# Attention, soft mixture of experts and a feed-forward block on one core: q and k loaded eight tokens to a partition, one head on each half of the partitions

## The chip, the core and the metric

The kernel runs on one core of a Trainium2 chip. A time is the device time of one execution, in microseconds (us), and the figure of a kernel is the median of its runs. Profiles are of one execution each. TensorE is PE below (PEld its weight loads), VectorE DVE, ScalarE ACT, GpSimd POOL, and SP is the queue that issues every DMA of this kernel.

## What is computed

Three blocks follow one another, all in float32: attention inside chunks of 64 tokens (8 batches, 8 heads, 576 tokens, head size 64), a soft mixture of 8 experts with 4 slots each, and a feed-forward block whose activation is the softplus.

```python
scores = scale * np.matmul(q_c, k_c.transpose(0, 1, 2, 4, 3))   # per chunk of 64
scores = scores - np.max(scores, axis=-1, keepdims=True)
attn = np.exp(scores)
attn = attn / (np.sum(attn, axis=-1, keepdims=True) + 1e-09)
out = np.matmul(attn, v_c)
...
logits = x @ phi                       # x: 4608 x 512
d = np.exp(logits - logits.max(0, keepdims=True))   # over the tokens
d /= d.sum(0, keepdims=True) + 1e-09
slot_input = d.T @ x                   # 8 experts x 4 slots x 512
slot_out[e] = np.maximum(slot_input[e] @ w1[e], 0.0) @ w2[e]
c = np.exp(logits - logits.max(1, keepdims=True))   # over the slots
c /= c.sum(1, keepdims=True) + 1e-09
x = c @ slot_out
...
h = x @ w_in
g = np.maximum(h, 0.0) + np.log1p(np.exp(-np.abs(h)))
out = g @ w_out
```

## The kernel before

**Units and loads.** The 4608 tokens are nine groups of 512, and a group has four units, each of two heads. A pair of units (`pr`, 18 of them) shares one load of q and one of k: 512 tokens of four heads, 1 MB for both. A batch has 576 tokens, so a group may lie across a batch boundary. `runs` (line 286) then cuts it in two pieces, whose first token in the group is a multiple of 64. Groups 0 and 8 are not cut, group 4 is cut into 256 and 256 tokens, the other six unevenly (64+448, 128+384, 192+320 and the reverse). `load_q` (line 295) issues one DMA for each piece of q and of k. In its tile `[128, 4, 4, D]` a partition holds four tokens of each of the four heads, so one packet is 4 x 64 floats, 1 KB, and 512 tokens fill all 128 partitions; a piece of 64 tokens fills 16 of them. There are two buffers each for q and k, and three for v, whose load (`load_v`, line 303) goes in packets of 256 bytes.

**A unit's steps.** `st_A` (line 424) turns one head's q and k: two transposes of 128x128 for each, every one over two tokens of each partition, into one bank of PSUM. `st_B` copies that bank on ACT into the tile `T` (line 442), in which the head has its 64 rows and the tokens stand in order. `st_S` (line 455) takes the scores of a chunk from `T`; softmax, the product with v, its transposes and the logits against `phi` follow. While this runs, the feed-forward weights `w_in` are loaded and rounded on DVE and POOL, and some expert weights are loaded ahead.

**What sets the order.** Every step of attention is given to `issue` (line 131), a small planner: it has a table of costs by engine (`COST`, line 106) and of buffers (`BUF`), and writes the steps out in the order in which its own clock would start them. That order is then fixed on every engine, SP's queue among them. `COST` has 3.4 for a load of q and k and 0.55 for a step `st_A`. A DMA on the queue waits until the buffer is free (the last transposes of the load two before), and until the DMA eight places ahead of it has landed, since eight semaphores go round. After attention the expert weights stream through the same queue (`hps` and `sops` are the two products), and the feed-forward block runs from a table of steps written out by hand (`MID`).

```python
# line 428 to 433, one head's transposes
for rr in range(2):
    nc.tensor.transpose(
        o[:, rr, :], t[:, 2 * (u % 2) + h, 2 * rr:2 * rr + 2, :].rearrange(
            "p r d -> p (r d)"), ident)
```

Of the kernel before, what the change touches and what calls it, by code (L numbers as in the profile page):

```python
# [8 lines left out]
F32 = mybir.dt.float32  # L9
# [174 lines left out]
def kernel(  # L184
# [12 lines left out]
    nc = tc.nc  # L197
    B, H, S, D = q.shape
# [21 lines left out]
    ident = const.tile([128, 128], F32, name="ident")  # L220
# [54 lines left out]
    rp_ = raw_ctx.enter_context(tc.tile_pool(name="raws", bufs=1, reuse_waits="tile"))  # L275
# [10 lines left out]
    def runs(t0, n):  # L286
        done = 0
        while done < n:
            b, s = divmod(t0 + done, S)
            step = min(n - done, S - s)  # L290
            yield done, step, b, s
            done += step


    def load_q(src, t, pr, hs=range(4)):
        G, h0 = pr // 2, 4 * (pr % 2)
        for off, n, b, s in runs(G * GT, GT):
            nc.sync.dma_start(
                out=t[off // 4:(off + n) // 4, hs[0]:hs[-1] + 1],
                in_=src[b, h0 + hs[0]:h0 + hs[-1] + 1, s:s + n, :].rearrange(  # L300
                    "h (p r) d -> p h r d", r=4))

    def load_v(t, pr):
        G, h0 = pr // 2, 4 * (pr % 2)
# [95 lines left out]
    def tr_tile(i):  # L400
        return psa.tile([128, 512], F32, tag=f"tr{i}", name=f"tr{i}")
# [3 lines left out]

    def st_l(pr):
        def f(e, held):
            ts = [rp_.tile([128, 4, 4, D], F32, tag=f"{nm}{held[nm, pr]}", name=nm)
                  for nm in "qk"]
            V["qk", pr] = ts  # L410
            for hs in (range(4),) if pr else (range(2), range(2, 4)):
                for src, t in zip((q, k), ts):
                    load_q(src, t, pr, hs)
        return f
# [9 lines left out]
    def st_A(u, h):  # L424
        def f(e, held):
            p = V["A", u, h] = tr_tile(held["tr", ("A", u, h)]).rearrange("x (i t) -> x i t", i=2)
            for i, t in enumerate(V["qk", u // 2]):
                o = p[:, i].rearrange("x (p rr) -> x rr p", rr=2)
                for rr in range(2):
                    nc.tensor.transpose(  # L430
                        o[:, rr, :], t[:, 2 * (u % 2) + h, 2 * rr:2 * rr + 2, :].rearrange(
                            "p r d -> p (r d)"), ident)
        return f

    def st_B(u, h):
# [228 lines left out]
    for u in range(NU):  # L664
        G, hp = divmod(u, HP)
        pr = u // 2
# [38 lines left out]
    for i in range(16):  # L705
        r = 2.0 * i + 3
# [21 lines left out]
    for i, (c, nms_, sls) in enumerate(ends):  # L728
# [4 lines left out]
        for sl in sls:  # L733
            n = next(n for n in home_of if home_of[n] == sl)
# [18 lines left out]
    for a in range(4):  # L753
# [5 lines left out]
        out=phi, in_=moe_phi.rearrange("(k p) s -> p k s", p=128)), rank=2.5)  # L759
# [9 lines left out]
        out=nM[:, 0], in_=nmr.rearrange("p g s -> p s g"), axis=AX.X, op=ALU.min)  # L769
# [10 lines left out]
        out=rep4w, in0=rep4[:, 0, :], scalar1=wc, scalar2=None, op0=ALU.mult)  # L780
# [22 lines left out]
    for kt in range(KD):  # L803
        nc.tensor.matmul(
            out=sp[:, kt, :], lhsT=acc[:, kt * 128:(kt + 1) * 128], rhs=rep4w,
# [119 lines left out]
    hps = psh.tile([128, 2, 512], F32, name="hps")  # L925
# [293 lines left out]
```

## Time and profile before

| what | value |
|---|---|
| median of 3 runs | 726.34 us (725.5 to 728.25) |
| the profiled execution | 725.14 us, its span 723.4 us |
| mean granted clock of TensorE | 0.969 |
| PE busy | 653.4 us (90%) |
| PE weight loads | 514.9 us (71%) |
| DVE busy | 414.4 us (57%) |
| ACT busy | 345.6 us (48%) |
| POOL busy | 336.7 us (47%) |
| DMA | 89.06 MB in 85440 packets |

A share of busy time is a mean over the whole span, in which the blocks follow each other with different loads on the engines; so the page's 40 slices (18 us each) come first, then the same table for chosen stretches. A matmul's busy time includes its way through the array, so a row of matmuls is read by the times at which they start. "DMA share" is the mean busy share of the 16 DMA engines; it goes over 1 because packets overlap. 1 GB/s is 1 KB per us.

### The profile page before, as it was taken

Reading aid. Unit: us, or ns where it says so; the run is one execution under the profiler, and the core shown is the slowest. Engines: PE = TensorE matmul, PEld = TensorE weight load, DVE = VectorE, ACT = ScalarE, POOL = GpSimd, SP = SyncE. Lnnn points to the kernel's source line nnn. Section 1 sums busy time; section 2 is a strip of 40 time slices with the busy share of each in tenths; the row PEclk is TensorE's granted clock in tenths of the full one; section 3 lists DMA queues with packets and bytes.
Section 4 is the critical chain, followed back from the end, with each engine's and each line's share of the span. In section 5 each row is a group of like instructions: output and inputs, shape, how many; then the busy total and the mean of one; then the engine's idle time right before and its main releaser. Section 6 shows DMA issues by size and latency. Waiting matters only on the chain.

```text
span 723.4 us, 14073 instructions
## 1 busy us (share of the span) xinstructions
PE 653.4 (90%) x5811; PEld 514.9 (71%) x5811; DVE 414.4 (57%) x598; ACT 345.6 (48%) x526; POOL 336.7 (47%) x222
## 2 busy tenths in 40 slices
PE   7779768878689687999999999999999999999997
PEld 6666556766444354877778888888888888888886
DVE  2768668778748558798785544444444444444430
ACT  5879667778522334465445333333333333333340
POOL 3647556556222423868755444434443433333340
PEclk9999999999979999999999999999999999999999
DMA  9999999999989993000002111000010010100101
GB/s 238 231 225 259 212 217 241 257 234 289 381 317 376 390 396 122 1 1 0 1 0 59 43 46 30 30 13 17 30 30 29 1 30 29 30 1 29 30 30 29
DMA packets 85440, 89.06 MB, mean 123 GB/s; under 512 B 41856, under 2 KB 60288, under 8 KB 85376
## 3 DMA queue, kind: packets, MB, share of 16 engines
q1 hardware_dynamic: 85376, 88.16, 43.8%
q8 instruction: 46, 0.75, 0.5%
q14 instruction: 18, 0.15, 0.1%
HBM read 78.71 MB, written 9.44 MB: 122 GB/s over the span
## 4 chain that ended last, share of the span: by engine, by line
PE 62%; DMA 15%; DVE 8%; issue 5%; ACT 4%; POOL 4%; SPq 1%; POOLq 0%; ACTq 0%; DVEq 0%
PE trm L1143 15%; PE trm L1141 15%; PE trm L1145 15%; DMA k<-in_k_dram 9%; PE ph L1090 4%; DMA w6b<-in_moe_w_dram 3%; PE tr L430 3%; ACT T L442 2%; PE hps L938 2%; DMA w3b<-in_moe_w_dram 1%; PE X L507 1%; PE S L455 1%; DMA vb<-in_v_dram 1%; POOL cvl L380 1%; PE tr L542 1%
## 5 line engine op out<-in xcount | busy, mean ns | idle before, releaser
L1124 POOL TENSOR_TENSOR g<-hTm,g 128x1024 fp32r<-128x1024 f32 (+1 forms) x48 | 112.7, 2348 | 143.7 <-ACT g L1120 143.7
L1109 ACT ACTIVATE hTm<-hTm 128x1024 f32<-128x1024 f32 (+2 forms) x51 | 51.5, 1010 | 160.3 <-DVE hTm L1103 160.3
L1103 DVE TENSOR_SCALAR hTm<-ph 128x1024 uint32<-128x1024 uint32 (+2 forms) x51 | 59.0, 1159 | 84.7 <-PE ph L1090 84.7
L442 ACT COPY T<-tr 64x512 f32<-64x512 f32 x144 | 90.2, 626 | 28.6 <-PE tr L430 26.7
L1124 POOL TENSOR_TENSOR g<-siT,g 128x1024 fp32r<-128x1024 f32 x24 | 58.1, 2422 | 62.3 <-ACT g L1120 62.3
L380 POOL TENSOR_TENSOR cvl<-cvl,cve 128x512 f32<-128x512 f32 x30 | 40.6, 1355 | 94.9 <-DVE cve L364 70.6
L1113 DVE SCALAR_TENSOR_TENSOR hTm<-ph,hTm 128x1024 f32<-128x1024 f32 (+2 forms) x51 | 59.1, 1159 | 39.6 <-ACT hTm L1109 39.6
L1109 ACT ACTIVATE siT<-siT 128x1024 f32<-128x1024 f32 x24 | 25.5, 1061 | 85.1 <-DVE siT L1103 85.1
L1090 PEld LDWEIGHTS ph<-cT,Tc 128*128 128x128 f32 x288 | 44.1, 191 | 17.0 <-issue 3.8
L1103 DVE TENSOR_SCALAR siT<-ph 128x1024 uint32<-128x1024 uint32 x24 | 29.3, 1222 | 42.9 <-PE ph L1090 42.9
L1090 PE MATMUL ph<-cT,Tc 128*128 128x256 f32 x288 | 47.8, 287 | 6.3 <-DVE hTm L1113 2.5
L1120 ACT CAST g<-hTm 128x1024 fp32r<-128x1024 f32 (+2 forms) x51 | 50.3, 988 | 2.2 <-DVE hTm L1113 2.2
L430 PE MATMUL tr<-ident,k 128*128 128x128 f32 x144 | 31.0, 300 | 14.3 <-DMA k<-in_k_dram 13.0
L1113 DVE SCALAR_TENSOR_TENSOR siT<-ph,siT 128x1024 f32<-128x1024 f32 x24 | 29.3, 1222 | 20.3 <-ACT siT L1109 20.3
L382 POOL TENSOR_TENSOR cvl<-cvl,cva 128x512 f32<-128x512 f32 x28 | 36.7, 1313 | 8.4 <-DVE cvl L380 6.5
L430 PE MATMUL tr<-ident,q 128*128 128x128 f32 x144 | 32.0, 307 | 8.5 <-DMA q<-in_q_dram 6.4
L549 DVE COPY xT<-tr 128x512 f32<-128x512 f32 x36 | 24.7, 686 | 20.8 <-PE tr L542 20.5
L467 DVE TENSOR_REDUCE nm<-S 128x8 f32<-128x512 f32 x36 | 24.8, 688 | 17.5 <-PE S L455 16.9
L455 PE MATMUL S<-T 64*64 64x64 f32 x1152 | 27.6, 234 | 6.6 <-DVE P L473 3.7
L430 PEld LDWEIGHTS tr<-ident,k 128*128 128x128 f32 x144 | 19.5, 155 | 17.4 <-DMA k<-in_k_dram 8.8
L542 PE MATMUL tr<-ident,x 128*128 128x128 f32 x144 | 24.1, 293 | 7.3 <-ACT T L442 3.8
L455 PEld LDWEIGHTS S<-T 64*64 64x64 f32 x1152 | 23.2, 146 | 9.8 <-issue 5.3
(364 smaller groups left out, 1730.3 us busy)
## 6 DMA issues: line engine op xcount, KB each, us to landing
g<-in_moe_w_dram SPq DMA_DIRECT2D x12, 1024.0 KB, 10.8
vb<-in_v_dram SPq DMA_DIRECT2D x64, 128.0 KB, 7.2
d<-in_moe_w_dram SPq DMA_DIRECT2D x5, 1024.0 KB, 13.7
out_dram<-ts SPq DMA_DIRECT2D x18, 256.0 KB, 2.1
out_dram<-ts SPq DMA_DIRECT2D x36, 128.0 KB, 2.3
w0a<-in_moe_w_in_dram SPq DMA_DIRECT2D x8, 512.0 KB, 5.9
w0b<-in_moe_w_in_dram SPq DMA_DIRECT2D x8, 512.0 KB, 7.1
q<-in_q_dram SPq DMA_DIRECT2D x4, 448.0 KB, 6.6
```

What stands on the lines that cost most here:

```text
L430: nc.tensor.transpose(o[:, rr, :], t[:, 2 * (u % 2) + h, 2 * rr:2 * rr + 2, :].rearrange("p r d -> p (r d)"), ident)
L442: on(e)(out=t[64 * h:64 * h + 64, :, r2, :], in_=p[64 * r2:64 * r2 + 64])
L455: nc.tensor.matmul(out=sp[64 * o:64 * o + 64, b, 64 * i:64 * i + 64], lhsT=qT[64 * h:64 * h + 64, cs], rhs=kT[64 * h:64 * h + 64, cs], sta ...
L1090: nc.tensor.matmul(out=ph(n, a, b)[:, j - a, :], lhsT=K["Tc"][:, f * 128:(f + 1) * 128], rhs=K["cT"][:, t * TT:(t + 1) * TT], start=True, ...
L1103: nc.vector.tensor_scalar(out=scratch(n, a, b).bitcast(U32), in0=ph(n, a, b).bitcast(U32), scalar1=0x80000000, scalar2=None, op0=ALU.bitwi ...
L1109: nc.scalar.activation(out=y, in_=y, func=AF.Softplus)
L1113: nc.vector.scalar_tensor_tensor(out=y, in0=ph(n, a, b), scalar=0.0, in1=y, op0=ALU.max, op1=ALU.add)
L1120: nc.scalar.copy(out=V["gs", n][:, 0, a:b], in_=scratch(n, a, b))
L1124: tt(eng)(out=s[:, 1, a:b], in0=scratch(n, a, b), in1=s[:, 0, a:b].bitcast(F32), op=ALU.subtract)
L1141: nc.tensor.matmul(out=po, lhsT=s[:, 0, j, ts_], rhs=wr[:, hs], start=(n in begin and j == 0), stop=False)
L1143: nc.tensor.matmul(out=po, lhsT=s[:, 0, j, ts_], rhs=wr[:, ls], start=False, stop=False)
L1145: nc.tensor.matmul(out=po, lhsT=s[:, 1, j, ts_], rhs=wr[:, hs], start=False, stop=(j == 3 and (n in part_end or n in sum_end)))
```

## The change

q and k stand in the tile `[128, 2, 8 * D]`. A partition holds eight tokens of two heads, one of each of the load's two units; the first head of each unit (`h = 0`) is on partitions 0 to 63, the second on 64 to 127. A packet is 8 x 64 floats, 2 KB. `load_q` issues two DMAs for each piece, one for each half. `st_A` turns one head with four transposes for q and four for k, each of 64 partitions and 128 columns against a 64x64 identity. The columns of the PSUM bank mean the same tokens as before, so all later steps are as they were. The planner's costs are as before, and so is the order in which it writes the steps.

```diff
-    def load_q(src, t, pr, hs=range(4)):
+    def load_q(src, t, pr, hps=range(2)):
         G, h0 = pr // 2, 4 * (pr % 2)
+        hs = slice(hps[0], hps[-1] + 1)
         for off, n, b, s in runs(G * GT, GT):
-            nc.sync.dma_start(
-                out=t[off // 4:(off + n) // 4, hs[0]:hs[-1] + 1],
-                in_=src[b, h0 + hs[0]:h0 + hs[-1] + 1, s:s + n, :].rearrange(
-                    "h (p r) d -> p h r d", r=4))
+            for h in range(2):
+                p0 = 64 * h + off // 8
+                nc.sync.dma_start(
+                    out=t[p0:p0 + n // 8, hs],
+                    in_=src[b, h0:h0 + 4, s:s + n, :].rearrange(
+                        "(hp h) (p r) d -> h p hp (r d)", h=2, r=8)[h, :, hs])
...
     def st_l(pr):
         def f(e, held):
-            ts = [rp_.tile([128, 4, 4, D], F32, tag=f"{nm}{held[nm, pr]}", name=nm)
+            ts = [rp_.tile([128, 2, 8 * D], F32, tag=f"{nm}{held[nm, pr]}", name=nm)
                   for nm in "qk"]
             V["qk", pr] = ts
-            for hs in (range(4),) if pr else (range(2), range(2, 4)):
+            for hs in (range(2),) if pr else (range(1), range(1, 2)):
...
             for i, t in enumerate(V["qk", u // 2]):
-                o = p[:, i].rearrange("x (p rr) -> x rr p", rr=2)
-                for rr in range(2):
+                o = p[:, i].rearrange("x (p rr) -> x rr p", rr=4)
+                hs = slice(64 * h, 64 * h + 64)
+                for rr in range(4):
                     nc.tensor.transpose(
-                        o[:, rr, :], t[:, 2 * (u % 2) + h, 2 * rr:2 * rr + 2, :].rearrange(
-                            "p r d -> p (r d)"), ident)
+                        o[:, rr, :], t[hs, u % 2, 128 * rr:128 * rr + 128], ident[hs, hs])
```

SP's queue before, at the load of the fourth pair (group 1, cut 64+448) with the `w_in` load behind it; a size is partitions x heads x floats, and `DMAHW0` to `DMAHW7` are the eight DMA semaphores:

```order
L298 DMA q<-in_q_dram 16x4x256 [waits DMAHW2_49,PE_49]
L298 DMA q<-in_q_dram 112x4x256 [waits DMAHW3_49]
L298 DMA k<-in_k_dram 16x4x256 [waits DMAHW4_49,PE_49]
L298 DMA k<-in_k_dram 112x4x256 [waits DMAHW5_49]
L341 DMA w0a<-in_moe_w_in_dram 128x1024 [waits DVE_49,DMAHW6_49,Activation_49,Pool_49]
```

The same place of the queue now:

```order
L302 DMA q<-in_q_dram 8x2x512 [waits DMAHW4_49,PE_49]
L302 DMA q<-in_q_dram 8x2x512 [waits DMAHW5_49]
L302 DMA q<-in_q_dram 56x2x512 [waits DMAHW6_49]
L302 DMA q<-in_q_dram 56x2x512 [waits DMAHW7_49]
L302 DMA k<-in_k_dram 8x2x512 [waits DMAHW0_49,PE_49]
L302 DMA k<-in_k_dram 8x2x512 [waits DMAHW1_49]
L302 DMA k<-in_k_dram 56x2x512 [waits DMAHW2_49]
L302 DMA k<-in_k_dram 56x2x512 [waits DMAHW3_49]
L345 DMA w0a<-in_moe_w_in_dram 128x1024 [waits DVE_49,DMAHW4_49,Activation_49,Pool_49]
```

Each transfer has become two, of half the partitions that it had, and the load goes once round the eight semaphores. In all, 66 transfers of q and k become 132.

Before, the same queue at group 4, whose loads were cut in the middle, each piece on one half of the partitions:

```order
L298 DMA q<-in_q_dram 64x4x256 x2
L298 DMA k<-in_k_dram 64x4x256 x2
L307 DMA vb_111<-in_v_dram 128x4x64 x4
L341 DMA w0b<-in_moe_w_in_dram 128x1024
```

PE before, at the first scores (S) and the transposes of the next unit (`tr` is the PSUM bank; a size is that of the output):

```order
L455 MATMUL S<-T 64x64 x32
L430 MATMUL tr_234<-ident,q 128x128 x2
L430 MATMUL tr_234<-ident,k 128x128 x2
L488 MATMUL tr_241<-ident,P 128x128 x4
L430 MATMUL tr_251<-ident,q 128x128 x2
L430 MATMUL tr_251<-ident,k 128x128 x2
```

The same place now:

```order
L459 MATMUL S<-T 64x64 x32
L435 MATMUL tr_256<-ident,q 128x64 x4
L435 MATMUL tr_256<-ident,k 128x64 x4
L492 MATMUL tr_267<-ident,P 128x128 x4
L435 MATMUL tr_277<-ident,q 128x64 x4
L435 MATMUL tr_277<-ident,k 128x64 x4
```

Nothing has changed its place; each head has eight transposes of half the width instead of four, 576 in all instead of 288.

## Rows read from the trace of the kernel before

**Rows 1.** The page's 40 slices of the span, in tenths; GB/s moved.
```profile
PE   7779768878689687999999999999999999999997
...
PEclk9999999999979999999999999999999999999999
DMA  9999999999989993000002111000010010100101
GB/s 238 231 225 259 212 217 241 257 234 289 381 317 376 390 396 122 1 1 0 1 0 59 43 46 30 30 13 17 30 30 29 1 30 29 30 1 29 30 30 29
```

**Rows 2.** Three stages: stretch, length, busy us (instructions) by engine, PEclk, DMA share, GB/s.
```profile
0.00:180.00 180.00, 142.11 (x2912) 112.64 (x2913) 125.57 (x273) 135.94 (x249) 100.85 (x102) 0.93 1.05 240
180.00:277.00 97.00, 75.85 (x870) 42.85 (x872) 62.75 (x125) 33.59 (x68) 31.55 (x25) 0.90 1.00 372
277.00:723.40 446.40, 435.47 (x2035) 359.39 (x2027) 226.05 (x202) 176.02 (x211) 204.29 (x96) 1.00 0.08 22
```

**Rows 3.** Line 430, the transposes of q and k: PE idle before it, until what.
```profile
its engine sat idle before it (us, times) until:
  DMA k<-in_k_dram: 21.8, 18
...
  DMA q<-in_q_dram: 10.0, 10
```

**Rows 4.** The same columns as rows 2, the 160 us inside attention.
```profile
20.00:180.00 160.00, 127.21 (x2706) 99.90 (x2699) 118.77 (x262) 123.80 (x230) 94.75 (x74) 0.94 1.06 240
```

**Rows 5.** Stretches with the packets of an uncut load (groups 0 and 8).
```profile
1.80:7.10 5.30, 4.00 (x19) 3.24 (x17) 0.00 (x0) 1.42 (x3) 2.31 (x15) 1.00 0.98 252
8.80:11.90 3.10, 1.07 (x34) 0.74 (x32) 1.32 (x2) 3.02 (x6) 0.00 (x0) 1.00 1.08 372
163.60:168.20 4.60, 3.81 (x106) 2.88 (x106) 4.36 (x10) 4.28 (x9) 4.35 (x4) 1.00 1.15 335
171.30:176.30 5.00, 3.84 (x33) 2.34 (x33) 4.78 (x10) 4.88 (x9) 1.14 (x1) 1.00 0.99 279
```

**Rows 6.** The two loads of group 4, each piece on one half of the partitions.
```profile
73.60:80.30 6.70, 4.02 (x106) 2.87 (x106) 4.25 (x11) 4.27 (x7) 6.14 (x5) 1.00 1.16 204
83.30:90.50 7.20, 6.10 (x145) 4.28 (x141) 5.30 (x13) 5.67 (x14) 3.12 (x3) 0.92 1.14 217
```

**Rows 7.** First and last of the twelve unevenly cut loads, and their sum.
```profile
15.30:22.10 6.80, 5.28 (x133) 4.35 (x135) 5.22 (x12) 6.38 (x12) 1.36 (x1) 0.94 1.06 252
...
151.10:157.40 6.30, 5.95 (x143) 4.51 (x138) 5.50 (x15) 4.87 (x12) 2.98 (x3) 0.87 1.10 236
sum 79.00, PE 64.89 PEld 50.52 DVE 63.20 ACT 63.84 POOL 46.21; mean PE 5.41 PEld 4.21 DVE 5.27 ACT 5.32 POOL 3.85
```

**Rows 8.** Line 298, the issues of q and k: ns min/median/max, and time to landing.
```profile
L298 SPq DMA_DIRECT2D k<-in_k_dram x33: 314/459/1618, 1.2 to 169.7; - x33
...
DMA to landing us min/median/max: 2.9/6.9/11.0
```

**Rows 9.** Timeline of PE's weight loads, one head's transposes: start, us, line, count.
```profile
92.36 0.25 PEld L430 LDWEIGHTS tr<-ident,q 128*128 128x128 f32 x2
92.58 0.25 PEld L430 LDWEIGHTS tr<-ident,k 128*128 128x128 f32 x2
92.80 0.47 PEld L542 LDWEIGHTS tr<-ident,x 128*128 128x128 f32 x4
```

**Rows 10.** Timeline of PE's weight loads between attention and experts.
```profile
206.97 1.36 PEld L743 LDWEIGHTS tr<-ident 128*128 128x128 f32 x6
208.21 1.83 PEld L804 LDWEIGHTS trm<-rep4w,acc 128*128 128x128 f32 x8
```

**Rows 11.** The granted clock (PEclk) at these two places, columns of rows 2.
```profile
208.30:210.10 1.80, 1.80 (x10) 1.73 (x9) 0.00 (x0) 0.00 (x0) 0.00 (x0) 0.50 1.04 385
92.30:92.80 0.50, 0.50 (x7) 0.50 (x5) 0.50 (x2) 0.41 (x2) 0.41 (x2) 1.00 0.86 269
```

**Rows 12.** The page's count of DMA packets.
```profile
DMA packets 85440, 89.06 MB, mean 123 GB/s; under 512 B 41856, under 2 KB 60288, under 8 KB 85376
```

## The prediction

> **What bounds the kernel now.** I read the page's slices first [rows 1]: DMA stands at 9 for the first 13 of 40 slices and near zero after the 16th, while PE is at 7 to 8 in the first part and at 9 in the second. A table of three stages says the same in times [rows 2]: attention, 0 to 180 us, with the DMA share at 1.05 and 240 GB/s; the expert weights, 180 to 277 us, at 1.00 and 372 GB/s; the feed-forward part, 277 us to the end, with PE busy 435.47 of 446.40 us and DMA at 0.08. So the first two stages run at the pace of DMA and the last at the pace of PE, and because the same queue carries attention and then weights, a microsecond of DMA won or lost in attention moves everything behind it.
>
> What attention waits for shows in the line that turns q and k [rows 3]: PE stood idle ahead of it 21.8 us for k and 10.0 us for q, 31.8 us in all. In the 160 us from 20 to 180 PE is busy 127.21 us [rows 4]; nearly all of the rest is that wait. PE is second, close behind DMA.
>
> The rate differs from load to load, and this decides the case. I cut the stage into the 18 stretches in which the packets of one q and k load (1 MB) ran. Four loads, of groups 0 and 8, meet no batch boundary: one piece over all 128 partitions. Leaving out the first, which starts an empty queue, and the last, which ends the stage, they run at 372 and 335 GB/s, all traffic counted [rows 5]. The two loads of group 4 are cut in the middle, so that each piece fills one half of the partitions: 64 and 64. They run at 204 and 217 GB/s [rows 6], 211 in the mean, with the DMA engines not less busy (1.16 and 1.14): the same bytes kept them busy longer. The other twelve are cut unevenly, 16+112 to 48+80 partitions; over 79.0 us they run at 210 to 256, in the mean 235 GB/s [rows 7].
>
> **The change, part by part.** *Half the partitions for each transfer.* In the new layout every q and k transfer fills at most 64 partitions, one half for each head, the form that group 4 has now. I take its 211 GB/s for all loads.
> - Four uncut loads: 252x5.3 + 372x3.1 + 335x4.6 + 279x5.0 = 5,425 KB in 18.0 us; at 211 GB/s 25.7 us: **+7.7**.
> - Two loads of group 4: **0**.
> - Twelve uneven loads: 18,570 KB in 79.0 us; at 211 GB/s 88.0 us: **+9.0**.
>
> The Trainium skill has a rule against this change (SBUF — State Buffer, "Can I just issue two DMAs to hit both halves?"): two transfers, one to each half of the partitions, gained 6% over one alone, and only a single transfer over all 128 reaches full rate. Its figures for 1 MiB, 196 GB/s into 64 partitions against 328 into 128, have a ratio of 0.60. The trace's 211 to 335 is 0.63, so the trace agrees; by the page's ratio the first item would be about +12 as an estimate.
>
> *Narrower pieces.* The uneven loads now go in pieces of 8+56 to 24+40 partitions, two of each. No row shows a piece under 16 partitions. From below this adds nothing. From above an uneven cut of a half costs as much again as the step from whole to half: 235 x 211/335 = 148 GB/s, 125.5 us, +37.5 over the 88.0. Rows 7 begin and end with loads cut 16+112, now at 252 and 236 GB/s: a narrow piece beside a wide one did less harm than the even cut. So I take a quarter: **+9.4**. In this bound lies also the queue: each transfer waits for the one eight places ahead to land, as the program's order shows, and a cut load now takes all eight places, against four.
>
> *Longer packets.* q and k go in 9,216 packets of 2 KB instead of 18,432 of 1 KB; nothing is added or taken for that. The whole-width load at 372 GB/s carried 1 KB packets, the weights with packets of 2 KB and more run at the same 372 [rows 2, 5]: from below it wins nothing. What it could win at most is in the faster rival.
>
> *Issues.* SP issues 132 q and k transfers instead of 66; at the median of a k issue, 459 ns [rows 8], that is +30 us on its queue. A transfer lands 6.9 us after its issue in the median, so SP is well ahead of the data, and DMA's own backlog hides it: **0**; if that cover went, 30 us over 18 loads would be 1.7 each.
>
> *PE.* Each unit has 16 transposes instead of 8, 288 more in all, each with 64 rows and 128 columns of weights and 64 columns moved instead of 128. Now four come every 0.44 us, 0.11 each (weight loads at 92.36, 92.58 and 92.80) at the full clock [rows 9, 11]. From below half the moving columns make each half as long and the sum stays. From above each keeps 0.11. The upper one is right if the 128-column weight load sets the pace, and two neighbours show that: at the granted clock 0.50 the warm-up matmuls with 128 columns moved take 1.36/6 = 0.23 us each, those of line 804 with only 32 moved 1.83/8 = 0.23 [rows 10, 11]. So 288 x 0.11 = +31.7 us of PE. It is hidden by the 31.8 us that PE now waits for q and k, a cover that grows by what DMA loses. Behind the last landing there is none: the last pair's 16 extra transposes are 1.8 us, and about **+1** of them lies on the path. The copies from PSUM, the scores and all later stages are as before.
>
> Sum: 7.7 + 9.0 + 9.4 + 1 = +27 us. The profiled execution took 725.1 us (span 723.4): 752. The median of the runs, 726.3, lies 1.2 above it: **753 us**.
>
> **The rivals.** *A: narrow pieces cost much more.* If the uneven cut halves again at nearly the full ratio, the sum is 7.7 + 9.0 + 37.5 + 1.8 = 56, up to 782 us. For it: every cut seen costs rate. Against it: the narrow-cut loads of rows 7. Here belongs a rule of the Trainium skill (DMA: Bandwidth & Descriptors, "Why a DMA increments its semaphore by 16 and not by 1"): a transfer runs on as many engines, up to 16, as divide its partition count. By it, pieces of 8, 24, 40 and 56 partitions would use 8, 12, 10 and 14 engines, and the lowest engines would get 17% more than their share; on the 25.7 + 13.9 + 88.0 us of all loads that is some +22 us as an estimate, between the forecast and A. All counts before divide by 16, so no row here shows it.
>
> *B: the halves run beside each other.* If the pieces fall out of step, so that one half is written while the other is too, DMA loses nothing. Then PE, with 31.7 us more work against 31.8 us of waits, holds the stage where it is: 723 to 730, about 727. Against it: in group 4, where the next piece of the other half was queued directly behind, no overlap shows.
>
> *C: faster.* Halves overlap as in B, all loads run at the uncut 335 GB/s, and the transposes are paced by their 64 moving columns. Group 4 and the uneven loads would take (2,930 + 18,570)/335 = 64 instead of 93 us: -29, which PE can follow only if its new work stays below some 15 us; with half of that price 711 us, 700 to 722. It decides in attention: loads above 250 GB/s and the transposes' pace under 0.08. Rows 6 and 10 speak against both.
>
> *That the change doesn't do what it says* would show as packets that stay at 1 KB: the count under 2 KB stays at 60,288 [rows 12] instead of falling to about 42,000. The order of the queue, with transfers of 64x2x512, leaves no room for that.
>
> **How the numbers follow.** About 0.5% (3.6 us) is what a measurement can tell from no change. Forecast, 740 to 765: 0.55. A, 765 to 783: 0.24. B: 0.10. C: 0.11. Slower is the forecast and A, 0.79; B lies within 0.5%, 0.10; C is faster, 0.11. The range leaves out C and the top of A: 725 to 783; the likeliest case's own is 740 to 765.
>
> **What would show it.** Right: attention's DMA goes on to about 205 instead of 180 us with slices near 211 GB/s, also in groups 0 and 8, still at a share of 1; PE is 30 us busier there; the two later stages keep their 97 and 446 us. The first step is wrong if the loads of groups 0 and 8 stay above 300 GB/s; the second if those of groups 1 to 3 and 5 to 7 run well above or below 190; PE's is wrong if its transposes come at 0.06 us each, or if PE rather than q and k is what attention waits for. The whole is wrong if attention ends by 180 us.

## The result, and the profile after

The change takes 737.14 us (median; 735.23 to 740.03), the kernel before 727.3 us beside it (725.5 to 730.31): ratio 1.0127 with a 95% interval of 1.0084 to 1.0171, or +9.2 us (+6.1 to +12.4). It is slower, as forecast, and inside the range of 725 to 783, but under the likeliest case's 740 to 765: the forecast was +27, three times as much. The profiled execution took 736.14 us, its span 734.4. Ratios, here and below, leave out the runs that lie more than 1.5% above the fastest of their kernel (three of x7's twelve) and differ from the quotients of the medians by up to 0.4%.

The slices of the changed kernel, which answer to [rows 1], and its count of packets, to [rows 12]:

```profile
PE   7688887878979868999899999999999999999997
...
PEclk9987989898878999999999999999999999999999
DMA  8999999989999996000001121001010010000101
GB/s 200 204 201 216 226 257 221 255 227 243 268 389 369 389 387 269 1 1 0 1 0 40 47 59 29 29 1 29 29 29 1 29 29 30 21 9 29 29 29 29
DMA packets 76962, 89.10 MB, mean 121 GB/s; under 512 B 42592, under 2 KB 42592, under 8 KB 76896
```

The stage of the expert weights (369 to 389 GB/s) begins a slice later and the rest is only shifted. The packets did become 2 KB: none is left between 512 B and 2 KB. The stages and the 160 us inside attention, to be read against [rows 2, 4]:

```profile
0.00:180.00 180.00, 146.84 (x2980) 117.58 (x2983) 118.79 (x254) 127.16 (x233) 96.62 (x98) 0.89 0.94 224
180.00:277.00 97.00, 81.10 (x1047) 47.26 (x1044) 62.84 (x128) 35.70 (x71) 30.94 (x24) 0.86 1.02 358
277.00:734.40 457.40, 443.80 (x2088) 364.95 (x2084) 235.09 (x217) 182.73 (x223) 209.31 (x100) 1.00 0.10 31
20.00:180.00 160.00, 131.33 (x2802) 104.17 (x2803) 113.82 (x246) 116.78 (x217) 90.54 (x71) 0.87 0.96 228
```

Inside attention DMA moved 228 GB/s in place of 240, at a share of 0.96 in place of 1.06. By 180 us attention was not done, so the last two stretches hold its rest as well. The forecast had a share that stays and a rate that falls, that is, engines that work more slowly; here they also rest more. The loads one by one, to be read against [rows 5 to 7]: first the three uncut ones whose packets can be told from the others' (the third of the four runs into 1 MB of expert weights in packets of the same size), then the two of group 4, then the first and last of eight uneven ones:

```profile
2.10:7.50 5.40, 4.08 (x23) 3.44 (x22) 0.00 (x0) 1.22 (x2) 2.03 (x13) 1.00 0.69 200
9.60:15.20 5.60, 3.49 (x71) 2.83 (x71) 2.66 (x4) 3.37 (x6) 0.00 (x0) 1.00 1.05 235
...
181.40:188.90 7.50, 6.85 (x70) 4.27 (x71) 4.43 (x9) 5.42 (x10) 1.51 (x2) 0.60 1.09 227
...
83.50:88.30 4.80, 4.80 (x121) 3.97 (x121) 4.29 (x10) 3.98 (x7) 2.92 (x3) 0.84 0.82 224
92.70:98.70 6.00, 3.81 (x88) 2.49 (x88) 5.79 (x12) 5.07 (x10) 4.23 (x4) 1.00 1.00 251
```
```profile
18.90:25.40 6.50, 4.94 (x141) 4.10 (x134) 4.76 (x12) 4.56 (x8) 2.43 (x2) 1.00 0.86 197
...
159.30:165.00 5.70, 3.52 (x88) 2.34 (x80) 5.23 (x10) 4.41 (x8) 5.38 (x5) 1.00 0.90 235
```

The uncut loads fell to 200 to 235 GB/s, where 211 was forecast. The eight uneven ones run at 184 to 235, 207 in the mean, over 53.5 us in place of 51.4. On PE, the idle time before line 435, the transposes of q and k, to be read against [rows 3]:

```profile
  DMA k<-in_k_dram: 23.0, 17
  issue: 15.6, 24
  DMA q<-in_q_dram: 9.0, 7
```

That is 32.0 us for q and k, as before (31.8). But both sums put together what PE and its weight loads each stood idle, as the waits between 20 and 180 us before, and between 20 and 190 us now, show (us, times, longest):

```profile
PE tr L430 <- DMA k<-in_k_dram: 12.6, 10, 2.1
PEld tr L430 <- DMA k<-in_k_dram: 8.2, 6, 2.2
PE tr L430 <- DMA q<-in_q_dram: 5.2, 6, 1.4
```
```profile
PE tr L435 <- DMA k<-in_k_dram: 12.9, 9, 2.4
PEld tr L435 <- DMA k<-in_k_dram: 7.3, 4, 2.5
PE tr L435 <- DMA q<-in_q_dram: 6.3, 4, 2.4
```

Where both stood idle at once, the time is counted twice. With each moment counted once, the trace has 23.1 us before and 22.2 now. Loads are still what attention waits for.

### The profile page after: what moved, and what is told of

Read it like the earlier page. It is cut to its first block, busy times and chain, and to the rows that moved or that the text cites. A ratio compares the mean times of both kernels' runs of the same rounds, so it can differ in the third digit from the quotient of the medians.

```text
span 734.4 us, 14742 instructions
## 1 busy us (share of the span) xinstructions
PE 671.7 (91%) x6099; PEld 529.8 (72%) x6099; DVE 416.7 (57%) x598; ACT 345.6 (47%) x526; POOL 336.9 (46%) x222
## 3 DMA queue, kind: packets, MB, share of 16 engines
q1 hardware_dynamic: 76896, 88.17, 42.3%
## 4 chain that ended last, share of the span: by engine, by line
PE 64%; DMA 14%; DVE 10%; issue 3%; ACT 3%; SPq 3%; POOL 2%; POOLq 0%; DVEq 0%; ACTq 0%
PE trm L1147 15%; PE trm L1145 15%; PE trm L1149 15%; DMA k<-in_k_dram 7%; PE ph L1094 4%; PE tr L435 3%; DMA w6b<-in_moe_w_dram 3%; SPq L302 2%; PE X L511 2%; PE hps L942 2%; PE tr L546 2%; PE tr L492 2%; PE S L459 2%; DMA vb<-in_v_dram 2%; DMA w3b<-in_moe_w_dram 1%
## 5 line engine op out<-in xcount | busy, mean ns | idle before, releaser
L435 PE MATMUL tr<-ident,k 64*128 64x64 f32 x288 | 32.6, 249 | 14.1 <-DMA k<-in_k_dram 14.1
L435 PE MATMUL tr<-ident,q 64*128 64x64 f32 x288 | 35.6, 263 | 7.6 <-DMA q<-in_q_dram 6.7
L435 PEld LDWEIGHTS tr<-ident,q 64*128 64x128 f32 x288 | 27.3, 162 | 16.4 <-issue 8.8
L435 PEld LDWEIGHTS tr<-ident,k 64*128 64x128 f32 x288 | 27.3, 163 | 15.7 <-DMA k<-in_k_dram 8.9
L459 PE MATMUL S<-T 64*64 64x64 f32 x1152 | 29.1, 242 | 7.6 <-DVE P L477 3.7
L497 ACT COPY P<-tr 128x512 f32<-128x512 f32 x36 | 21.1, 587 | 31.2 <-PE tr L492 30.9
```

Of the source, the lines that this page charges most:

```text
L435: nc.tensor.transpose(o[:, rr, :], t[hs, u % 2, 128 * rr:128 * rr + 128], ident[hs, hs])
L459: nc.tensor.matmul(out=sp[64 * o:64 * o + 64, b, 64 * i:64 * i + 64], lhsT=qT[64 * h:64 * h + 64, cs], rhs=kT[64 * h:64 * h + 64, cs], sta ...
```

## Experiments

The change has two parts that can be had alone, the transposes and the loads, and the loads have two again: twice the number of transfers, and half the partitions for each. Thirteen kernels were run, each beside the kernel before, whose medians lay between 727.9 and 729.5 us; differences in us are the ratio times 728. Theories go by letters, which the expectations use: T, PE's added transposes; C, the granted clock; H, the halves of the partitions; Q, the number of transfers.

| run | us | ratio to before | interval |
|---|---|---|---|
| the change | 737.14 | 1.0127 | 1.0084 to 1.0171 |
| x1, transposes alone | 729.8 | 1.0017 | 0.9991 to 1.0042 |
| x2, loads alone | 738.54 | 1.0109 | 1.0050 to 1.0169 |
| x3, twice the transfers | 734.86 | 1.0078 | 1.0049 to 1.0107 |
| x4, uncut loads in halves | 733.8 | 1.0082 | 1.0049 to 1.0116 |
| x5, transposes twice | 729.63 | 1.0016 | 0.9987 to 1.0045 |
| x6, before, v in 18 transfers | 725.89 | 0.9953 | 0.9923 to 0.9983 |
| x7, the change, v in 18 transfers | 735.95 | 1.0051 | 1.0015 to 1.0087 |
| x8, q below, k above | 757.8 | 1.0376 | 1.0327 to 1.0425 |
| x9, the same by two heads | 736.67 | 1.0110 | 1.0081 to 1.0139 |
| x10, both halves in one | 798.35 | 1.0949 | 1.0901 to 1.0997 |
| x11, pause of 24 increments | 760.83 | 1.0436 | 1.0389 to 1.0483 |
| x12, pause of 7 increments | 728.64 | 1.0007 | 0.9980 to 1.0034 |
| x13, uncut loads as before | 732.82 | 1.0063 | 1.0028 to 1.0097 |

**PE or the loads?** x1 has before's loads and the 16 transposes of 64 rows; x5 does each 128-row transpose twice (by the prediction's price PE's +31.7 us; by the pages PE is busy 674.0 us in place of 653.4); x2 has the change's loads with eight 128-row transposes.

```
x1: +hs = slice(64 * h, 64 * h + 64)
    ...
    +for y in range(2):
         nc.tensor.transpose(
    -        o[:, rr, :], t[:, 2 * (u % 2) + h, 2 * rr:2 * rr + 2, :].rearrange(
    -            "p r d -> p (r d)"), ident)
    +        o[:, rr, 64 * y:64 * y + 64],
    +        t[hs, 2 * (u % 2) + h, 2 * rr:2 * rr + 2, :].rearrange(
    +            "p r d -> p (r d)"), ident[hs, hs])
x5: -for rr in range(2):
    +for rr in (0, 0, 1, 1):
x2: ...
    -o[:, rr, :], t[hs, u % 2, 128 * rr:128 * rr + 128], ident[hs, hs])
    +o[:, rr, :], t[:, u % 2, 128 * r4:128 * r4 + 128], ident)
```

> The loads of the kernel before, with the change's PE work alone: 16 transposes of 64 rows a unit, the first head of a unit from partitions 0 to 63 and the second from 64 to 127, each of them turned twice (so half of the tokens of q and k are left out and the other half stand twice). Theory T (PE: the longer transposes set attention back, the loads do not): 735 to 739 us, like the change, with DMA's share in attention falling under 1. Theory L (the loads in halves set it back and PE hides behind them): 726 to 729 us. Both at once, each a part: 730 to 734 us.

> The kernel before with every transpose of q and k done twice, 128 rows each time: 16 of 128x128 a unit, the same +31.7 us of PE at 0.11 us each, loads as before. Theory T in its plain form (PE time alone): the same as the run with 64 rows, 735 to 739 us. If what costs is the granted clock that falls with the 64-row form (theory C): 727 to 731 us here, with the mean granted clock in attention at 0.93 or more, against 0.87 in the change.

> The change's loads with PE's work of before: 8 transposes of 128 rows a unit, each over both halves of the partitions (so the columns of the scores are those of other tokens and heads than the reference pairs). Theory T: 724 to 729 us, as before or a little less. Theory L: 735 to 739 us, as the change. Each a part: 730 to 734 us.

x1 and x5 cannot be told from no change, x2 has the whole loss. The 160 us inside attention of x1, then of x5, and the idle time before the transposes of x5:

```profile
20.00:180.00 160.00, 135.45 (x2887) 106.15 (x2879) 115.86 (x255) 122.44 (x228) 90.58 (x71) 0.88 1.03 233
```
```profile
20.00:180.00 160.00, 143.15 (x2919) 121.79 (x2919) 117.52 (x259) 124.72 (x231) 91.24 (x72) 0.97 1.04 238
```
```profile
  DMA k<-in_k_dram: 8.6, 7
  issue: 5.7, 6
  DMA q<-in_q_dram: 3.9, 3
```

In x5 PE is busy 143.15 us in place of 127.21 [rows 4], and its waits for q and k shrink from 31.8 to 12.5 us, or, counted once, from 23.1 to 7.9: the added work moved into them, and the run's +1.1 us (-0.9 to +3.3) cannot be told from nothing. In x1 the granted clock stands at 0.88, as low as the change's 0.87, without loss. T and C fall.

**Halves or number?** x3 cuts each of before's 66 transfers in two by heads: 132 as in the change, but over the same partitions. x4 cuts only the uncut loads, into tokens 0 to 255 and 256 to 511, so to halves: step 1 of the prediction alone.

```
x3: ...
    +for g in (hs[0], hs[0] + w):
         nc.sync.dma_start(
    -        out=t[off // 4:(off + n) // 4, hs[0]:hs[-1] + 1],
    +        out=t[off // 4:(off + n) // 4, g:g + w],
    ...
x4: +for y in ((0, 256) if n == GT else (0,)):
    ...
    -        out=t[off // 4:(off + n) // 4, hs[0]:hs[-1] + 1],
    +        out=t[(off + y) // 4:(off + y + m) // 4, hs[0]:hs[-1] + 1],
    ...
```

> The kernel before with every q and k transfer cut in two by heads: 132 transfers instead of 66, each over the same partitions as before, packets of 1 KB, PE as before. If the eight places of the DMA queue or SP's issues matter (theory Q): 731 to 738 us. If not: 726 to 729 us, with the burst rates of the uncut loads above 330 GB/s as before.

> The kernel before, with only the uncut transfers of q and k (token groups 0 and 8, ten of the 66) cut into 256 tokens each, so that each goes to partitions 0 to 63 or 64 to 127; the shape, the packets of 1 KB and the transposes stay. This is step 1 of the prediction alone. Theory H (a transfer to half of the partitions moves at the 211 GB/s of group 4, so these loads take longer): +7.7 us, about 736. Theory Q (the number of transfers counts: SP's queue holds a transfer back until the one eight places ahead has landed, and doubling the 66 transfers cost 6.8 us): 10 x 6.8 / 66 = +1.0 us, about 729.

Both cost: x3 +5.7 us (3.6 to 7.8), x4 +6.0 (3.6 to 8.4). And they do so in different ways. Here are x3's 160 us and its time from issue to landing, against 240 GB/s, 1.06 and 6.9 us before [rows 4, 8]:

```profile
20.00:180.00 160.00, 118.95 (x2519) 93.13 (x2523) 109.81 (x240) 115.72 (x216) 90.14 (x70) 0.93 0.92 226
...
DMA to landing us min/median/max: 2.1/4.7/8.9
```

The engines of DMA are less busy: too little is on its way. (Each transfer also lands sooner, as it would by its half size alone.) The four uncut loads of x4, against [rows 5]:

```profile
2.30:8.50 6.20, 4.09 (x16) 2.68 (x15) 0.00 (x0) 1.22 (x2) 1.85 (x12) 1.00 0.71 196
9.80:15.20 5.40, 3.73 (x54) 3.05 (x56) 1.38 (x2) 4.12 (x7) 0.00 (x0) 1.00 1.09 238
167.00:173.80 6.80, 4.08 (x106) 3.04 (x106) 4.20 (x10) 4.20 (x8) 5.75 (x5) 1.00 1.19 220
176.90:183.40 6.50, 6.22 (x88) 4.85 (x82) 4.36 (x12) 5.40 (x12) 0.00 (x0) 0.69 1.13 227
sum 24.90, PE 18.11 PEld 13.62 DVE 9.95 ACT 14.94 POOL 7.60; mean PE 4.53 PEld 3.40 DVE 2.49 ACT 3.74 POOL 1.90
```

24.9 us in place of 18.0, +6.9 (the same four loads, uncut, took 17.7 to 20.4 us in the profiles of x1, x3, x5, x6, x12 and x13), and in the last three the engines are as busy as before or busier at 220 to 238 GB/s in place of 279 to 372: here they work more slowly. So H holds for the uncut loads, and Q's +1.0 for them is too little.

**What is left of the uneven loads?** x13 has the change's loads but leaves the uncut ones as they were; its transposes are those of x2.

```
+if n == GT:
+    nc.sync.dma_start(
+        out=t.rearrange("p a (b x) -> p (a b) x", b=2)[:, 2 * hps[0]:2 * hps[-1] + 2],
+        in_=src[b, h0 + 2 * hps[0]:h0 + 2 * hps[-1] + 2, s:s + n, :].rearrange(
+            "h (p r) d -> p h (r d)", r=4))
+    continue
...
```

> The change's loads without its uncut ones: the uncut loads of q and k (token groups 0 and 8) go to all 128 partitions with 1 KB packets, ten transfers, as in the kernel before; the other 56 are doubled to 112, to halves, with 2 KB packets, as in the change. Eight 128-row transposes a unit, whose columns are of other tokens and heads. These are steps 2 and 3 of the prediction without step 1: by the prediction +9.0 + 9.4 = +18.4 us, about 746. Theory I (issue time on SP, 56 more at 0.10 us) without any cost of halves on the uneven loads: +3 to +6 us, 731 to 734. If the whole loss sits here and halves cost nothing: +9 us, 737.

+4.6 us (2.0 to 7.1), a quarter of the +18.4 that steps 2 and 3 gave. The uncut loads are back, as its four stretches show; then the sum over the eight uneven loads whose packets can be told apart, and for the same eight loads the sum of the kernel before:

```profile
1.80:6.50 4.70, 3.92 (x18) 3.26 (x17) 0.00 (x0) 1.06 (x3) 2.29 (x15) 1.00 0.95 271
7.40:11.70 4.30, 3.16 (x42) 2.50 (x40) 0.99 (x2) 2.98 (x5) 0.00 (x0) 1.00 1.03 316
172.10:176.90 4.80, 2.97 (x102) 2.23 (x94) 4.13 (x9) 3.40 (x7) 4.56 (x4) 1.00 1.12 315
...
sum 54.30, PE 42.74 PEld 33.50 DVE 43.73 ACT 42.65 POOL 30.90; mean PE 5.34 PEld 4.19 DVE 5.47 ACT 5.33 POOL 3.86
```
```profile
sum 51.40, PE 44.57 PEld 35.24 DVE 41.22 ACT 42.11 POOL 27.32; mean PE 5.57 PEld 4.41 DVE 5.15 ACT 5.26 POOL 3.42
```

The eight loads take 2.9 us more. For twelve that would be +4.4, close to the run's +4.6, but that proves nothing: 2.6 of the 2.9 us are one load's, 7.2 us in place of 4.6, and this load took 7.4 and 6.9 us in x4 and x12, whose uneven loads are before's. In the profiles of x1, x4, x5, x6 and x12 the same eight, unchanged, took 48.7 to 52.3 us. What stands is the run's time. x4 and x13 together make +10.6, the change +9.2.

**What is it in the number that costs?** Fewer transfers should win. v goes in 80 transfers; x6 (on the kernel before) and x7 (on the change) load it with 18.

```
-for m in range(4):
-    for off, n, b, s in runs(G * GT + 128 * m, 128):
-        nc.sync.dma_start(
-            out=t[off:off + n, m, :, 0:D],
-            in_=v[b, h0:h0 + 4, s:s + n, :].rearrange("h p d -> p h d"))
+rows = v.rearrange("b h s d -> (b h s) d")[2048 * pr:2048 * pr + 2048]
+nc.sync.dma_start(out=t.rearrange("p m h w -> p (m h) w")[:, :, 0:D],
+    in_=rows.rearrange("(x p) d -> p x d", p=128))
```

> The kernel before, with each of the 18 loads of v as one transfer of 2048 consecutive rows of v instead of four to six transfers (80 in all): the same bytes in pieces of 256 B, so that the values are those of other tokens and heads. q and k are as before. Theory Q (each transfer on SP's queue costs about 6.8 / 66 = 0.10 us while the loads bound the stage): 62 fewer, -6.4 us, about 722. Theory H (half of the partitions, not the number, is what cost): no change, 728.

> The change with each of the 18 loads of v as one transfer of 2048 consecutive rows (values of other tokens and heads), so that attention's loads of q, k and v are 150 transfers, against 146 in the kernel before and 212 in the change. Theory Q (the number of transfers): the loss is gone, 727 to 730. Theory H (halves of the partitions): the loss stays, 736 to 738. Between the two, 731 to 734: both have a part.

x6 won 3.4 us (1.2 to 5.6), about half of what Q gave. x7 stands at +3.7 (1.1 to 6.3) over before, or at +6.5 by the medians of all its runs, the change at +9.2 (6.1 to 12.4), each beside its own runs of before. That lies between the two theories, which speaks for a part of both; how large each is, x7 doesn't show. Two things hang on the number: the time that SP needs to issue, and the eight places on its queue. x11 and x12 add SP's time alone, as increments of a semaphore that nothing waits for.

```
         in_=src[b, h0 + hs[0]:h0 + hs[-1] + 1, s:s + n, :].rearrange(
             "h (p r) d -> p h r d", r=4))
x11: +for i in range(24):
x12: +for i in range(7):
     +    nc.sync.sem_inc(own, 1)
```

> The kernel before, with 24 increments of a semaphore that nothing waits for behind each of the 66 transfers of q and k on SP's queue, 17 ns each by the profile of before, 0.41 us together, about as long as the issue of one transfer (0.46 us median): SP's own time of 66 more issues, without the transfers. Theory I (SP's issue time is what the number of transfers costs): as the doubled transfers, +6 us, about 735, SP's waits for PE shorter than before's. Theory W (the eight places on the queue are what costs: a transfer waits until the one eight ahead has landed): no change, 728 to 730.

> As the run with 24 increments of a semaphore behind each of the 66 transfers of q and k, whose trace showed 60 ns each (1.43 us a pause, 94 us on SP's queue, +33 us), with 7: 0.42 us a pause, 28 us on the queue, what 66 more issues take (0.43 to 0.45 us each where the transfers were doubled). No transfer is added and none cut. Theory I (SP's own time is what the number of transfers costs): +4 to +7 us, 732 to 735, as with the doubled transfers. Theory W (the eight places, and smaller transfers in them): no change, 727 to 729.

The timeline of SP (start, length, line) in x11, then in x12, shows how long the pauses were:

```profile
0.73 0.44 SPq L300 DMA_DIRECT2D q<-in_q_dram  x1
2.66 0.39 SPq L300 DMA_DIRECT2D k<-in_k_dram  x1
```
```profile
0.74 0.45 SPq L300 DMA_DIRECT2D q<-in_q_dram  x1
1.68 0.38 SPq L300 DMA_DIRECT2D k<-in_k_dram  x1
...
20.00:180.00 160.00, 128.33 (x2658) 101.24 (x2659) 118.59 (x258) 122.12 (x227) 93.19 (x73) 0.91 1.05 238
```

From the end of one issue to the next lie 1.49 and 0.49 us; 0.06 of it was there before. x11's 24 increments so took 60 ns each, not the 17 ns that I had read: 66 x 1.43 = 94 us on SP, more than it can hide (+31.7 us, a run of the wrong size that says only where SP's slack ends). x12's 66 x 0.43 = 28 us are those of 66 more issues, and they cost +0.5 us (-1.5 to +2.5), with DMA at 1.05 and 238 GB/s. Theory I falls. What is left of Q's cost is in the transfers themselves: smaller pieces in a fixed number of places. That it is the places was not tried by itself, but x3's lower share speaks for it, and so do SP's own waits. Up to 195 us, on the lines that load q, k and v, SP waited 7.8 us for another transfer to land before, 3.3 in x12, 17.0 in x3 and 26.5 in the change. The largest such row, before and in x3:

```profile
SPq L307 <- DMA q<-in_q_dram: 2.5, 5, 0.8
SPq L309 <- DMA q<-in_q_dram: 4.6, 9, 0.9
```

**Why do the halves cost 6 us and not more?** x8 keeps 66 transfers but gives each to a half, q below and k above, and turns both together with eight 128-row transposes a unit; x9 cuts these transfers in two by heads, so that the halves take turns in pieces of at most 256 KB in place of 512.

```
x8: -out=t[off // 4:(off + n) // 4, hs[0]:hs[-1] + 1],
    +out=t[64 * i + off // 8:64 * i + (off + n) // 8, hs[0]:hs[-1] + 1],
    ...
x9: -for hs in (range(4),) if pr else (range(2), range(2, 4)):
    +for hs in (range(2), range(2, 4)):
```

> The 66 transfers of before, not 132, but each to half of the partitions: q of eight tokens to a partition on 0 to 63, k on 64 to 127, packets of 2 KB as in the change, and the same uneven numbers of partitions; eight 128-row transposes a unit turn q and k together. Theory H (half of the partitions, or fewer DMA engines on each transfer, is what costs): as the loads of the change alone, +10 us, about 738; if only what is left of them over the doubled transfers, +3 to +4, about 732. Theory Q (only the number of transfers counts): no change, 727 to 729, and a DMA share of 1.0 or more between 20 and 180 us.

> As the run with q on partitions 0 to 63 and k on 64 to 127 (757.8 us with 66 transfers), but each transfer cut in two by heads, so that the two halves alternate in pieces of at most 256 KB in place of 512 KB, as in the change: 128 transfers. Theory G (what a half costs hangs on how long the DMA engines write to one half before the other: the shorter the alternate pieces, the less): faster than with 66 transfers, by 10 us or more, 738 to 748. Theory Q (each transfer more costs 0.10 us, and the size of the pieces nothing): 62 more, +6 us, about 764.

x8 costs +27 us, x9 +8.0. Their 160 us, x8 first:

```profile
20.00:180.00 160.00, 115.10 (x2353) 93.22 (x2346) 102.01 (x225) 106.78 (x199) 79.97 (x64) 0.87 1.03 204
```
```profile
20.00:180.00 160.00, 120.81 (x2593) 97.98 (x2593) 111.62 (x246) 116.85 (x217) 90.28 (x70) 0.91 0.98 225
```

x8's engines are busy (1.03) and move 204 GB/s; x9's are less busy and move more. Q, which gave x9 another +6, falls as the only cause, and G's forecast came: with shorter turns on the halves most of the loss is gone. (x9 also lets the first unit of a load start on half of it; how much of the gain that is stays open.) But, as far as the stretches tell, it came in the cut loads alone. The first five uneven ones took 42.3 us in x8, 35.2 in x9 and 31.7 before. Of the uncut ones, the three whose packets can be told apart took 18.4 us in x8, 17.4 in x9, 18.1 in x4 and 13.4 before: turns of 256 KB gave them next to nothing back. The Trainium skill (SBUF — State Buffer, "Can I just issue two DMAs to hit both halves?") says that two transfers to the two halves serialize. x4 and x8 agree with that; x9, 19 us under x8, shows that for the cut loads the size of the pieces decides what it costs.

**Can one transfer have both halves?** x10 carries the two heads of a unit with one transfer to 128 partitions, for the uncut loads.

```
+if n == GT:
+    for hp in hps:
+        nc.sync.dma_start(out=t[:, hp],
+            in_=src[b, h0 + 2 * hp:h0 + 2 * hp + 2, s:s + n, :].rearrange(
+                "h (p r) d -> h p (r d)", r=8))
+    continue
```

> The change, but for the uncut loads (token groups 0 and 8) one transfer carries the two heads of a unit to both halves, 128 partitions, packets of 2 KB: 16 transfers in place of 20; all others stay as in the change, 128 in all. Theory H (step 1 of the prediction, halves on the uncut loads, +6.0 measured by itself): 6 us are gone, about 731 to 732, what then stays is the number of transfers. Theory Q (only the number counts): 4 fewer of 132, nothing seen, 736 to 738.

798.35 us, +69: neither theory. Its first 20 us, and its count of packets:

```profile
0.00:20.00 20.00, 4.78 (x23) 4.14 (x24) 0.17 (x1) 2.49 (x3) 3.49 (x26) 1.00 0.15 50
```
```profile
DMA packets 76674, 89.10 MB, mean 112 GB/s; under 512 B 42304, under 2 KB 42304, under 8 KB 76608
```

DMA stands at a share of 0.15, about 2 of 16 engines, and the small packets, one for each engine of a transfer among them, are 288 fewer than in the change: 20 transfers x 16 = 320 gone, 16 x 2 = 32 in their place. The source's outermost dimension is the two heads, and by these counts two engines did the work. It says nothing on halves.

No version that puts every value in its place beats the kernel before; x6, which does by 3.4 us, puts v's rows in other places.

## Why the prediction was right and wrong

- **What bounds attention, and the stages behind it**: right. Loads are waited for as before, and the end moved by what attention lost. Its last q and k came in at 188.9 us (176.3 before), where about 205 was forecast.
- **Uncut loads in halves, +7.7**: right in size. +6.0 by x4's time, at most +6.9 by its stretches, and the rate fell to 196 to 238 GB/s.
- **Group 4, 0**: right as far as one profile tells: 10.8 us for both loads in place of 13.9, without four late packets.
- **Uneven loads at 211 GB/s, +9.0**: the rate came, the price did not. x13's eight loads ran at 190 to 221 GB/s, 206 in the mean, but took only 2.9 us longer. The step carried all the KB of a stretch over to the new rate; in fact the q and k of a load are 1 MB, and the other traffic in a stretch is not bound to it (11,188 KB are in x13's eight stretches, 11,955 in those of before). And the cause is another, at least in the main: in these stretches the mean share is 0.90 in place of 1.06, so the engines were not slower but less busy, as in x3 (0.86). Halves also had little to take here: x4's uncut loads in halves reach 220 to 238 GB/s, and the uneven ones ran at 235 before. By its size x13's loss could be all the number of transfers (56 of x3's 66 at 5.7 us are 4.8). But x3's own eight loads took 49.5 us, no longer than the 51.4 before, so that its loss lies for the most part between the loads, and x13's took 54.3; a part of the halves is neither shown nor excluded.
- **Narrower pieces, +9.4**: with the step before it, this is what failed. x13 holds both, and together they are +4.6 (2.0 to 7.1), not +18.4; it doesn't tell how the 4.6 divide. This step had no row behind it: it took a quarter of a bound that was made by applying the step from whole to half a second time. An uneven cut had already been in small pieces, and two small pieces to two halves take turns, as in x9, whose cut loads were faster than x8's.
- **The queue's eight places** were put into that bound in half a sentence. They, or whatever else in the number of transfers is not SP's time, have a price of their own (x3, +5.7), about what the uneven loads lost in all.
- **SP's 30 us of issues hidden**: right (x12, +0.5).
- **PE, +31.7 us, hidden**: hidden is right (x5), but the cover and the size were misread. The cover of 31.8 us counts the common waits of PE and its weight loads twice; it was 23.1. And by the pages PE is busy only 18.3 us longer (671.7 against 653.4). What of the +1 behind the last landing came can't be told in x1's +1.2 (-0.7 to +3.1). Weight loads of the changed kernel, and the clock there:

```profile
106.40 0.32 PEld L435 LDWEIGHTS tr<-ident,q 64*128 64x128 f32 x4 [0.17 <-DVE cve L368]
106.65 0.33 PEld L435 LDWEIGHTS tr<-ident,k 64*128 64x128 f32 x4
107.04 0.20 PEld L546 LDWEIGHTS tr<-ident,x 128*128 128x128 f32 x2
```
```profile
106.40:107.00 0.60, 0.60 (x9) 0.57 (x8) 0.50 (x2) 0.43 (x1) 0.60 (x1) 1.00 0.77 222
```

Four come in 0.25 us, 0.06 each at the full clock, half of [rows 9]: the lower bound. The prediction had taken the pace of a weight load from line 804 [rows 10], whose loads have 128 rows; these have 64. That row, with 32 columns moved at the pace of 128, speaks for the rows loaded and not the columns moved as what halved it; it was not tried.

- **The packets**: 2 KB as said. The Trainium skill (DMA: Bandwidth & Descriptors, "Why a DMA increments its semaphore by 16 and not by 1") has a transfer run on the largest number of engines up to 16 that divides its outermost dimensions, and the counts follow it (x10's 288; the change has 736 small packets more than before, where 66 x 16 would be 1,056). The +22 us that I had worked out from this rule did not come. Engines busy 0.96 left room for an uneven share, but no run shows what that costs by itself.
- **The rivals**: A is out, and so is C. B held in the main for the small pieces of the uneven loads, not for the uncut loads in pieces of 256 KB.

With the measured terms the sum is 6.0 + 4.6 = +10.6, inside the measured +6.1 to +12.4.

## What to carry to other kernels

Where a queue is the bound, look at its rate and its busy share together: a lower rate at the same share is engines that work more slowly (here: pieces of 256 KB and more to one half of the partitions), a lower rate at a lower share is too little on its way (here: twice as many transfers of half the size, +5.7 us for 66). A stretch's rate prices only its own bytes; traffic that ran beside them moves elsewhere, so compare how long the stretches last, and over more than one profile: eight loads that no edit touched took 48.7 to 52.3 us. The idle times of PE and of its weight loads lie over each other and don't add. Don't apply the same loss twice to get a bound for a case that no row shows.

## What the runs showed that was not expected

- A transfer whose source begins with a dimension of 2 ran on two engines, though it filled 128 partitions: 50 GB/s in the first 20 us, +69 us for 16 such transfers.
- Pieces of at most 256 KB that take turns on the two halves cost 19 us less than pieces of up to 512 KB (+8.0 against +27.4), with twice the transfers.
- Semaphore increments on SP came every 60 ns, though the row of SP's semaphore instructions at line 298 shows 17 ns for each.
